# Folding a weight by seven half-block products a row pair, with sums and adds on GpSimd

## The chip, the cores and the metric

The kernel runs on one core of one Trainium2 chip. The metric is the device time of one execution in microseconds; the profile is one such execution, with a span of its own from the first to the last instruction.

## The reference

An mLSTM cell over 4 batches, 8 heads, 768 steps and a head width of 40, followed by a multiplicative feed-forward block on the cell's output, seen as 3072 tokens of width 320. All data are float32.

```python
# cell, for every step t (state C, n, m per batch and head)
m_new = np.maximum(f_gate[:, :, t] + m, i_gate[:, :, t])
f_stab = np.exp(f_gate[:, :, t] + m - m_new)
i_stab = np.exp(i_gate[:, :, t] - m_new)
C = f_stab * C + i_stab * einsum('bhd,bhe->bhde', vt, kt)
n = f_stab * n + i_stab * kt
y[t] = sigmoid(o_gate[t]) * einsum('bhde,bhe->bhd', C, qt) / max(|n . qt|, 1)
# feed-forward, x = y as (3072, 320)
a = x @ w1          # 320 x 1024
b = x @ w2
h = a * b @ w3      # 1024 x 1024
out = h @ w_out     # 1024 x 320
```

There is no nonlinearity between w3 and w_out, so the kernel folds the two: w3o = w3 @ w_out, 1024 x 320, and out = (a * b) @ w3o.

## The kernel before

The cell works on 24 blocks of 128 tokens (6 blocks of time times 4 batches), one a step `s`; the feed-forward block is spread over the same steps and eight more. The loop at L820 runs 32 steps. In a step stand, in program order: loads, the state's first decay (`decayed`, L333, GpSimd), the transposition of an older block's output into `xT` (`x_trans`, L478: TensorE transposes, ScalarE copies it out of the bank at L486), products with the folded weight where due (`fold`, `ffn_out`), the `up` blocks (a and b for two of the eight row blocks of w1 and w2, 256 tokens each), and the cell itself (`quarter_work`, L338). In the cell TensorE runs `up_rest` (the last 64 rows of the width), then the products of the cell, the first of which is `ph`; VectorE follows with the gating, the state's sums (L404, L414) and the output y (L445); GpSimd does the second decay between L404 and L414, then the weighted values of the next step (`weighted`, L327) and its masks (L308). At the end of a step two or three pieces of w3 are converted from raw words to float32 and transposed by VectorE (`convert`, L237, with L199, L200 and L248), ScalarE scales the next raw pieces (`scale_next`, L191 and L195; from step 9 on it keeps two scaled ones ready, L971), and SyncE issues the next loads, the raw pieces last (L184). There are four raw buffers (L179) and two for transposed rows of w3 (`w3T`, L247).

`x_trans` lags three steps behind in this part: in step 10 it turns block 7, in 12 block 9, in 14 block 11. The `up` blocks of steps 10 and 11 read blocks 6 and 7, those of 12 and 13 blocks 8 and 9, those of 14 and 15 blocks 10 and 11.

The fold is made by rows. A row `ko` is 128 rows of w3, complete in `w3T` after two conversions; a step later `fold` (L253) calls `w3_mm` (L259): eight products of 128 x 128 by 128 x 320 into one bank, which ScalarE empties into `w3o[:, ko]` (L264). Rows 0 and 1 come in step 10, then one a step up to row 7 in step 16. In steps 16 to 20 two output blocks a step follow (`ffn_out`, L733), whose copies to `o_sb` and stores are ScalarE's.

What sets the order: `in_order` (L84) chains all of TensorE's instructions in the order in which they are written. For the other engines `keep_order` (L549), called at the end of the last step (L979), chains every instruction traced after the front to the one before it on its engine. So all queues follow the program's text. [...]

Two other parts of the kernel already work by seven products in place of eight half-block ones: `up_by_seven` (L668, from step 19) and `out_by_seven` (L772, at the end).

Of the kernel before, what the change touches and what calls it, by code (L numbers as in the profile page):

```python
# [8 lines left out]
FP = mybir.dt.float32  # L9
U32 = mybir.dt.uint32  # L10
AF = mybir.ActivationFunctionType
OP = mybir.AluOpType
UP = 2.0 ** 9
# [3 lines left out]
def kernel(  # L17
# [26 lines left out]
    nc = tc.nc  # L44

    B, H, S, D = q.shape
    L = 64
    P = 128
# [6 lines left out]
    DM = H * D  # L55
    BH = B * H
    DFF = moe_w1.shape[1]
    FO = DFF // P
# [6 lines left out]
    const = ctx.enter_context(tc.tile_pool(name="const", bufs=1))  # L65
    wst = ctx.enter_context(tc.tile_pool(name="wst", bufs=2))
# [10 lines left out]
    def mps(shape, name):  # L77
        pool = banks.pop(0)
        banks.append(pool)
        return pool.tile(shape, FP, name=name, tag="m")  # L80

    last = []
# [8 lines left out]
    def mm(out, lhsT, rhs, start=True, stop=True):  # L91
        in_order(nc.tensor.matmul(out, lhsT=lhsT, rhs=rhs, start=start, stop=stop))  # L92
# [75 lines left out]
    wo = const.tile([128, FO, DM], FP, name="wo")  # L168
# [3 lines left out]
    w3o = const.tile([128, FO, DM], FP, name="w3o")  # L172
    CW = 512
# [35 lines left out]
    pend, scaled = [], []  # L209
# [18 lines left out]


    w3T_t = {}  # L230
    turned_w3, ready_w3 = [], []

    def scale_next(early=False):
        scaled.append(pend.pop(0))
# [2 lines left out]
    def convert():  # L237
        if not scaled:
            scale_next()
        dst, raw, ko, half = scaled.pop(0)  # L240
        if dst is not None:
            to_f32(dst, raw)
            return
        w3 = wst.tile([128, CW], FP, name="w3", tag="w3")
        to_f32(w3, raw)
        if half == 0:
            w3T_t[ko] = wst.tile([128, FO, 128], FP, name="w3T", tag="w3T")  # L247
        nc.vector.transpose(out=w3T_t[ko].rearrange("c k (m r) -> c m k r", r=32)[:, 2 * half:2 * half + 2],  # L248
                            in_=w3.rearrange("r (m c k) -> r m k c", m=2, k=FO))
        if half:  # L250
            turned_w3.append(ko)

    def fold():  # L253
        while ready_w3:
            w3_mm(ready_w3.pop(0))
        ready_w3.extend(turned_w3)
        turned_w3.clear()

    def w3_mm(ko):  # L259
        w3T = w3T_t.pop(ko)  # L260
        wp = mps([128, DM], "wp")
        for ki in range(FO):
            mm(wp, w3T[:, ki, :], wo[:, ki, :], start=(ki == 0), stop=(ki == FO - 1))
        nc.scalar.mul(out=w3o[:, ko, :], in_=wp, mul=UP ** -2)  # L264


    qT_t, kT_t, vw_t, before_t, y_t, x_t = {}, {}, {}, {}, {}, {}
# [227 lines left out]
    f_sb, a, F, U, on = (gates[0:RG, i * TC:(i + 1) * TC] for i in range(5))  # L495
# [99 lines left out]
    for i, r in enumerate(third):  # L595
        nc.gpsimd.tensor_tensor(out=pick[r, :, i, :], in0=pair[r].to_broadcast([BH, B * NP, GC]), op=OP.mult,
                        in1=dec[r].unsqueeze(1).to_broadcast([BH, B * NP, GC]))
# [15 lines left out]
    ffn = ctx.enter_context(tc.tile_pool(name="ffn", bufs=2))  # L613


    ab_t = {}

    def up(gr, fs, cs):


        if gr not in ab_t:
            ab_t[gr] = [ffn.tile([128, FO, 2 * P], FP, name="ab", tag="ab", bufs=6) for _ in range(2)]
        x, n = x_t[gr], cs.stop - cs.start
        pa, pb = mps([128, len(fs), n], "pa"), mps([128, len(fs), n], "pb")
        for p, wt in ((pa, w1), (pb, w2)):
            for i, f in enumerate(fs):
                for cc in range(KF):
                    mm(p[:, i, :], wt[:, cc, f * 128:(f + 1) * 128], x[:, cc, cs], start=(i == cc == 0), stop=False)
        return pa, pb, x, gr, fs, cs

    def up_rest(pa, pb, x, gr, fs, cs):
        for i, f in enumerate(fs):
            for j, e in quarters:
                mm((pa, pb)[j][halves[e], i, :], wr[halves[j], f * 128 + e * L:f * 128 + (e + 1) * L],
                   x[halves[j], KF, cs], start=False, stop=(i == len(fs) - 1))
        j, t0 = divmod(cs.start, 2 * P)
        a_sb = ffn.tile([128, len(fs), cs.stop - cs.start], FP, name="a_sb", tag="a_sb")
        nc.scalar.mul(out=a_sb, in_=pa, mul=UP ** -2)  # L638
        nc.vector.tensor_tensor(out=ab_t[gr][j][:, fs[0]:fs[-1] + 1, t0:t0 + a_sb.shape[-1]], in0=pb, in1=a_sb, op=OP.mult)  # L639
# [90 lines left out]

        return single, shared, left, product

    def ffn_out(blocks, pos=None):  # L733

        pos = pos or [mps([P, DM], "po") for _ in blocks]
        for (gr, j), po in zip(blocks, pos):
            for f in range(FO):
                mm(po, ab_t[gr][j // 2][:, f, j % 2 * P:(j % 2 + 1) * P], w3o[:, f, :], start=(f == 0), stop=(f == FO - 1))
        for (gr, j), po in zip(blocks, pos):
            o_sb = ffn.tile([P, DM], FP, name="o_sb", tag="o_sb", bufs=2)  # L740
            nc.scalar.copy(out=o_sb, in_=po)  # L741
            t0 = j * S + gr * P
            nc.scalar.dma_start(out=out[t0:t0 + P, :], in_=o_sb)


    KH, NH = FO // 2, DM // 2

    def out_weight_sums():

        T_o.extend(m[:, i * KH * NH:(i + 1) * KH * NH].rearrange("p (f n) -> p f n", n=NH)  # L750
                   for m, i in ((v_all, 0), (gates, 0), (gates, 1), (q_all, 0)))
        (B11, B12), (B21, B22) = ([w3o[:, k * KH:(k + 1) * KH, i * NH:(i + 1) * NH] for i in range(2)] for k in range(2))
        T1, T2, T3, T4 = T_o
        for dst, p, q in ((T1, B12, B11), (T2, B22, T1), (T3, B22, B12), (T4, B21, T2)):
            yield nc.gpsimd.tensor_tensor(out=dst, in0=p, in1=q, op=OP.subtract)

    T_o, S_o = [], {}
    wsums = out_weight_sums()

    def quarters_of_ab(gr, j):  # L760
        return [[ab_t[gr][j][:, k * KH:(k + 1) * KH, t * P:(t + 1) * P] for k in range(2)] for t in range(2)]
# [10 lines left out]
    def out_by_seven(gr, j, sums=None):  # L772
# [25 lines left out]
        for t in range(2):  # L798
# [3 lines left out]
    ups = [(gr, [f, f + 1], slice(j * 2 * P, (j + 1) * 2 * P)) for gr in range(3) for j in range(2)  # L802
           for f in range(0, FO, 2)]
    downs = [(gr, j) for gr in range(NG) for j in range(GT)][:14]
    outs = [(gr, j) for gr in range(3, NG) for j in range(2)][1:]
    summed = list(outs)
    sevens = [(gr, f) for gr in range(3, NG) for f in range(FH)]
    n_up = [0] * 2 + [1] * 4 + [2] * 10 + [0] * 16
    n_seven = [0] * 19 + [1] * 12 + [0]
    n_down = [0] * 16 + [2] * 5 + [1] * 4 + [0] * 7  # L810
# [9 lines left out]
    for s in range(len(n_up)):  # L820
# [28 lines left out]
        while s >= N_DVE and turned < min(s - 2, NY):  # L849
            x_trans(turned)  # L850
            turned += 1
        fold()
        if s >= len(n_up) - 2:
            ab_sums(*summed.pop(0))
        def pairs():
# [13 lines left out]
            seven[1]()  # L869
        if seven and s <= NU:  # L870
            ffn_out([downs.pop(0) for _ in range(n_down[s])], [cell[1][:, i, 0:DM] for i in range(2)])
        else:
            for _ in range(n_down[s]):
                ffn_out([downs.pop(0)])
# [2 lines left out]
        if seven and s > NU:  # L877
            seven[0]()
        now = [ups.pop(0) for _ in range(n_up[s])]
        open_ups = [up(*x) for x in now] if s != 2 else []  # L880
        if s == 3:
            turn(3)
        def rest():
            for x in open_ups:
                up_rest(*x)
            if seven:
                seven[2]()
            if s == 3:
                scale_next()
                scale_next()  # L890
# [23 lines left out]
        if s <= NU:  # L914
            gated = quarter_work(s, rest, between if s == 2 else None, convert if s == 3 else None)
        else:
            rest()
        with tc.issue_after(gated.ins) if gated else nullcontext():
            if seven:
                seven[3]()  # L920
            for _ in range({NU: 1, NU + 1: 3}.get(s, 0)):
                next(wsums)
            if s == NU + 1:
                ab_sums(*summed.pop(0))
            if NY <= s - 2 < NU:
                x_turn(s - 2)
            for n in () if s == 1 else (s + 2,) if s < B else (s + 2, s + 3) if s == B else (s + 3,):
                if n < N_U:
                    rows_of_u(n)
            if N_DVE <= s + 1 < NU:  # L930
                gated = turn(s + 1)
            if s - 2 in range(4 * GT - 1, NU, GT):
                token_sums((s - 2) // GT)
            if s < len(n_up) - 2 and n_out[s + 1] and s > NU + 2:
                ab_sums(*summed.pop(0))
# [28 lines left out]
        if s == B:  # L964
            for i, r in enumerate(third):
                nc.sync.dma_start(out=U_d[i * GC:(i + 1) * GC].rearrange("c r t -> r c t"), in_=U3[r])
        with tc.issue_after(gated.ins) if N_DVE <= s + 1 < NU else nullcontext():
            for _ in range(n_cvt[s] if s < len(n_cvt) else 0):
                convert()
                converted += 1  # L970
# [9 lines left out]
            for ins in keep_order(front):  # L980
                behind.enter_context(tc.issue_after(ins))
    behind.close()
    assert not ups and not sevens and not downs and not outs and not summed and not todo and not pend and not turned_w3 and not ready_w3, (len(ups), len(downs), len(todo), len(pend))
# [1 line left out]
_INS = ['q', 'k', 'v', 'i_gate', 'f_gate', 'o_gate', 'moe_w1', 'moe_w2', 'moe_w3', 'moe_w_out']  # L985
_OUTS = [((3072, 320), 'float32')]
# [25 lines left out]
```

## Time and profile before

| what | value |
|---|---|
| time, median of 3 runs | 427.91 us (426.82 to 428.42) |
| profiled execution | 427.89 us |
| its span | 425.8 us |
| granted clock, mean | 0.996 |
| ScalarE in a usual step (125.84 to 141.13 us, 15.29) | 6.50 us busy |
| VectorE in it | 12.24 us |
| GpSimd in it | 3.46 us |
| evacuation of a row of the fold (L264), 8 of them | 0.44 us each |

"PE" is TensorE's matmul row, "PEld" its weight loads, DVE VectorE, ACT ScalarE, POOL GpSimd, SP SyncE. A float32 product appears as two records. A record is drawn from its start to its modelled end, and records overlap, so the time that a group takes is read from the start of one group to the start of the next. "L92" is the line of the helper that all products go through; they are told apart by the names of what they write and read.

### The profile page before, as it was taken

What the parts mean: (1) busy time and instruction counts of PE and PEld (TensorE: products, weight loads), DVE (VectorE), ACT (ScalarE), POOL (GpSimd) and SP (SyncE); (2) the same over time, 40 slices, a digit from 0 to 9 for tenths busy, and PEclk for the clock granted to TensorE, in tenths of its full rate; (3) what the DMA queues carried; (4) which work ended last, traced back from release to release, by engine and by line L of the source; (5) the groups of instructions that cost most, each with busy time, mean ns of one, the idle gap of its engine ahead of it and who ended that gap; (6) DMA issues with size and microseconds to landing.
All of it is one profiled execution on the core that took longest, in us unless ns stands there. A gap on an engine that the chain in (4) does not pass through costs nothing.

```text
span 425.8 us, 13079 instructions
## 1 busy us (share of the span) xinstructions
PE 414.1 (97%) x5353; PEld 335.3 (79%) x5353; DVE 313.5 (74%) x635; ACT 150.1 (35%) x404; POOL 154.3 (36%) x211
## 2 busy tenths in 40 slices
PE   7989989999999999999999999999999999999996
PEld 4768878888688788787777778788778879888896
DVE  6676986888949779778736966596868699575971
ACT  4766865567723623630433313032311110210000
POOL 4421342233303303303307751546453587542100
PEclk9989999999999999999999999999999999999999
DMA  8999998598977776985425675756421120000001
GB/s 186 204 173 245 214 144 140 134 193 180 215 183 154 166 182 135 181 164 105 89 80 130 153 141 121 142 133 117 87 44 36 35 39 2 31 2 31 2 32 62
DMA packets 135211, 51.15 MB, mean 120 GB/s; under 512 B 109360, under 2 KB 126960, under 8 KB 135152
## 3 DMA queue, kind: packets, MB, share of 16 engines
q1 hardware_dynamic: 131552, 46.29, 53.9%
q10 hardware_dynamic: 3600, 4.03, 2.7%
q8 instruction: 42, 0.69, 0.7%
q14 instruction: 17, 0.14, 0.1%
HBM read 44.50 MB, written 5.80 MB: 118 GB/s over the span
## 4 chain that ended last, share of the span: by engine, by line
PE 53%; issue 20%; DVE 7%; POOL 7%; SPq 7%; DMA 5%; ACT 1%; POOLq 0%; DVEq 0%
PE cell L92 17%; PE pa L92 12%; PE o L92 8%; PE pb L92 8%; PE p L92 3%; POOL pw L308 3%; SPq L184 3%; DVE w3T L666 2%; PE pt L95 1%; POOL vw L330 1%; SPq L148 1%; DMA raw<-in_moe_w_dram 1%; PE fill L92 1%; POOL raw L659 1%; POOL state L335 1%
## 5 line engine op out<-in xcount | busy, mean ns | idle before, releaser
L335 POOL TENSOR_TENSOR state<-state,decay 128x164 f32<-128x164 f32 x40 | 20.0, 500 | 154.8 <-DVE state L404 129.0
L92 PE MATMUL pa<-xT,w 128*128 128x256 f32 x240 | 60.4, 382 | 0.0
L92 PEld LDWEIGHTS pa<-xT,w 128*128 128x128 f32 x240 | 44.4, 190 | 6.8 <-DVE h L430 0.4
L303 ACT ACTIVATE pw<-pw,aT 128x64 f32<-128x64 f32 x184 | 46.4, 339 | 3.2 <-ACT o_sb L741 1.9
L92 PE MATMUL pb<-xT,w 128*128 128x256 f32 x192 | 45.4, 379 | 0.0
L729 POOL TENSOR_TENSOR ab<-ab,a_sb 128x512 f32<-128x512 f32 x22 | 29.4, 1356 | 32.2 <-DVE ab L684 32.2
L92 PEld LDWEIGHTS pb<-xT,w 128*128 128x128 f32 x192 | 36.4, 190 | 5.0
L711 POOL TENSOR_TENSOR wo<-wo 128x512 f32<-128x512 f32 x22 | 27.4, 1268 | 29.8 <-DVE wo L686 29.8
L92 PE MATMUL pa<-xT,wr 64*64 64x256 f32 x384 | 37.0, 386 | 0.5 <-DVE wr L200 0.5
L92 PE MATMUL wp<-wo,w3T 128*128 128x320 f32 x128 | 35.9, 433 | 1.1 <-DVE ab L639 0.6
L308 POOL TENSOR_SCALAR_AFFINE_SELECT pw<-pw 64x512 f32<-64x512 f32 x48 | 35.8, 746 | 3.0 <-ACT pw L303 1.2
L92 PE MATMUL pb<-xT,wr 64*64 64x256 f32 x384 | 36.4, 380 | 0.0
L92 PE MATMUL cell<-w3o,ab 128*128 128x320 f32 x128 | 35.4, 432 | 0.0
L638 ACT ACTIVATE a_sb<-pa 128x512 f32<-128x512 f32 x24 | 14.3, 598 | 59.0 <-PE pb L92 59.0
L639 DVE TENSOR_TENSOR ab<-pb,a_sb 128x512 f32<-128x512 f32 x24 | 16.4, 688 | 23.2 <-ACT a_sb L638 22.8
L92 PEld LDWEIGHTS wp<-wo,w3T 128*128 128x128 f32 x128 | 23.8, 190 | 10.5 <-DVE ab L639 0.8
L92 PEld LDWEIGHTS cell<-w3o,ab 128*128 128x128 f32 x128 | 24.3, 190 | 9.5
L92 PEld LDWEIGHTS pa<-xT,wr 64*64 64x64 f32 x384 | 18.9, 132 | 15.4 <-issue 8.8
L686 DVE SCALAR_TENSOR_TENSOR a_sb<-pa,wo 128x512 f32<-128x512 f32 x12 | 8.3, 689 | 29.8 <-PE pa L92 29.8
L430 DVE TENSOR_TENSOR h<-cell,h 64x164 f32<-64x164 f32 x88 | 28.6, 326 | 1.6
L92 PE MATMUL po<-w3o,ab 128*128 128x320 f32 x96 | 26.4, 433 | 0.0
L92 PEld LDWEIGHTS po<-w3o,ab 128*128 128x128 f32 x96 | 18.1, 190 | 7.3
(180 smaller groups left out, 846.4 us busy)
## 6 DMA issues: line engine op xcount, KB each, us to landing
raw<-in_moe_w_dram SPq DMA_DIRECT2D x64, 128.0 KB, 3.4
kbuf<-in_k_dram SPq DMA_DIRECT2D x24, 160.0 KB, 4.5
v_all<-in_v_dram SPq DMA_DIRECT2D x24, 160.0 KB, 4.9
o_in<-in_o_gate_dram SPq DMA_DIRECT2D x24, 160.0 KB, 4.8
pw<-U_d SPq DMA_DIRECT2D x28, 128.0 KB, 3.5
raw<-in_moe_w_dram SPq DMA_DIRECT2D x5, 512.0 KB, 6.7
raw<-in_moe_w_out_dram SPq DMA_DIRECT2D x8, 320.0 KB, 4.1
gates<-in_k_dram SPq DMA_DIRECT2D x28, 80.0 KB, 2.5
```

What stands on the lines that cost most here:

```text
L92: in_order(nc.tensor.matmul(out, lhsT=lhsT, rhs=rhs, start=start, stop=stop))
L184: nc.sync.dma_start(out=dst, in_=src)
L303: nc.scalar.activation(out=pw[:, h, :], in_=src[:, h, :], func=AF.Exp, bias=aT[:, c, b * H + h:b * H + h + 1])
L308: nc.gpsimd.affine_select(out=pw[r], in_=pw[r], compare_op=OP.is_ge, fill=0.0, base=0, pattern=[[0, H], [1, L]], channel_multiplier=-1)
L335: nc.gpsimd.tensor_tensor(out=new, in0=old, op=OP.mult, in1=decay[:, b * NP:(b + 1) * NP, 2 * c + x:2 * c + x + 1] .to_broadcast([P, NP, D1]))
L430: nc.vector.tensor_tensor(out=part, in0=ph[x][halves[e]], in1=part, op=OP.add)
L638: nc.scalar.mul(out=a_sb, in_=pa, mul=UP ** -2)
L639: nc.vector.tensor_tensor(out=ab_t[gr][j][:, fs[0]:fs[-1] + 1, t0:t0 + a_sb.shape[-1]], in0=pb, in1=a_sb, op=OP.mult)
L666: nc.vector.tensor_tensor(out=dst, in0=p, in1=q, op=OP.subtract)
L686: nc.vector.scalar_tensor_tensor(out=out, in0=p, scalar=UP ** -2, in1=q, op0=OP.mult, op1=OP.add)
L711: aside_by.tensor_tensor(out=kept[j][:, 1:4:2], in0=kept[j][:, 1:3], in1=kept[j][:, 3:4].to_broadcast([128, 2, TH]), op=OP.add)
L729: aside_by.tensor_tensor(out=t[:, f:FO:FH, :], in0=t[:, f:FO:FH, :], in1=a, op=OP.mult)
```

## The change

The eight row products a row of w3 are replaced. Two rows (2i and 2i + 1) and the two column halves of w_out make a 2 x 2 by 2 x 2 product of blocks, and this is made with seven products of half blocks in place of eight. The sums of w_out's blocks (T1, T2, T4, and B22 - B12 in place of B12) are made once, those of a row pair (S1, S2, S4, and S3 in place of A21) for each pair, all on GpSimd, and so are the five adds that put the products together; ScalarE alone empties the banks.

- Steps 8 and 9: two sums of w_out each, on GpSimd, after the cell.
- Steps 9, 11, 13, 15: `fold_sums` of a pair on GpSimd after the cell; at the end of the step, ahead of the conversions, `fold_first`: two products and their emptying. In step 15 it also rebuilds T4 in B21's place.
- Steps 10, 12, 14: the first `up` of the step with its rest, then `fold_second`: the other five products and two emptyings; then the second `up`. The adds are issued on GpSimd after the cell.
- Step 16: `ffn_out` is split: six of the eight f for both blocks, then `fold_second(3)` with its adds, and after the cell the other two f and the stores.
- `w3` has one buffer in place of two; `o_sb` lies in the memory of T1; group 2's `ab` is taken in step 9, its memory serves the sums meanwhile; the last pair's sums use two raw buffers.

```diff
-        w3 = wst.tile([128, CW], FP, name="w3", tag="w3")
+        w3 = wst.tile([128, CW], FP, name="w3", tag="w3", bufs=1)
...
-    def w3_mm(ko):
-        w3T = w3T_t.pop(ko)
-        wp = mps([128, DM], "wp")
-        for ki in range(FO):
-            mm(wp, w3T[:, ki, :], wo[:, ki, :], start=(ki == 0), stop=(ki == FO - 1))
-        nc.scalar.mul(out=w3o[:, ko, :], in_=wp, mul=UP ** -2)
+    def fold_weight_sums():
+        (B11, B12), (B21, B22) = halves_of(wo)
+        T1, T2, T4 = (m.rearrange("p (f n) -> p f n", n=NH) for m in
+                      (fold_m[:, 0], fold_m[:, 1], w3o[:, FO - 2:FO].rearrange("p k n -> p (k n)")))
+        fold_T.extend((T1, T2, B12, T4))
+        for dst, p, q in ((T1, B12, B11), (T2, B22, T1), (T4, B21, T2), (B12, B22, B12)):
+            yield nc.gpsimd.tensor_tensor(out=dst, in0=p, in1=q, op=OP.subtract)
+
+    def fold_sums(i):
...
+        (A11, A12), (A21, A22) = rows_of_w3(i)
+        S1, S2, S4 = (m.rearrange("p (k r) -> p k r", r=128) for m in mem)
+        fold_S[i] = S1, S2, A21, S4
+        fold_M[i] = mem[1], mem[2]
+        for dst, p, q, op in ((S1, A21, A22, OP.add), (S2, S1, A11, OP.subtract), (A21, A11, A21, OP.subtract),
+                              (S4, A12, S2, OP.subtract)):
+            nc.gpsimd.tensor_tensor(out=dst, in0=p, in1=q, op=op)
+
+    def fold_first(i):
+        (A11, A12), _ = rows_of_w3(i)
+        (B11, _), (B21, _) = halves_of(wo)
+        wp = fold_products(((A11, B11), (A12, B21)))
+        if i == FO // 2 - 1:
+            nc.gpsimd.tensor_tensor(out=B21, in0=B21, in1=fold_T[1], op=OP.subtract)
+            fold_T[3] = B21
+        nc.scalar.mul(out=fold_of(i)[:, 0:3:2], in_=wp, mul=UP ** -2)
+
+    def fold_second(i):
...
+        wp, wq = mps([128, 3, NH], "wp"), mps([128, 2, NH], "wq")
+        for p, x, a, b, first, last in ((wq, 1, A22, T4, True, False), (wp, 0, S1, T1, True, False), (wp, 1, S2, T2, False, False),
+                                        (wp, 2, S3, T3, False, True), (wq, 0, S4, B22, False, True)):
+            for k in range(KH):
+                mm(p[:, x], a[:, k, :], b[:, k, :], start=(first and k == 0), stop=(last and k == KH - 1))
+        M1, M2 = (m[:, 0:n * NH].rearrange("p (x n) -> p x n", n=NH) for m, n in zip(fold_M[i], (3, 2)))
+        nc.scalar.mul(out=M1, in_=wp, mul=UP ** -2)
+        nc.scalar.mul(out=M2, in_=wq, mul=UP ** -2)
+
+        def adds():
+            for out, p, q in ((C[:, 1], M1[:, 1], C[:, 0]), (C[:, 0], C[:, 0], C[:, 2]), (C[:, 2], M1[:, 2], C[:, 1]),
+                              (C[:, 1:4:2], C[:, 1:3], M1[:, 0:1].to_broadcast([128, 2, NH])), (C[:, 1:3], M2, C[:, 1:3])):
+                nc.gpsimd.tensor_tensor(out=out, in0=p, in1=q, op=OP.add)
+        return adds
...
-        fold()
...
+        elif s == 16:
+            finish = ffn_out([downs.pop(0) for _ in range(n_down[s])], split=FO - 2)
+            fold_second(FO // 2 - 1)()
...
         now = [ups.pop(0) for _ in range(n_up[s])]
-        open_ups = [up(*x) for x in now] if s != 2 else []
+        open_ups, adds = [], []
+        if s in (10, 12, 14):
+            up_rest(*up(*now.pop(0)))
+            adds.append(fold_second((s - 10) // 2))
+        if s != 2:
+            open_ups = [up(*x) for x in now]
...
+        if s == 16:
+            finish()
         with tc.issue_after(gated.ins) if gated else nullcontext():
             if seven:
                 seven[3]()
+            if s in (8, 9):
+                next(fsums), next(fsums)
+            for x in adds:
+                x()
+            if s in (9, 11, 13, 15):
+                fold_sums((s - 9) // 2)
...
+        if s in (9, 11, 13, 15):
+            fold_first((s - 9) // 2)
         with tc.issue_after(gated.ins) if N_DVE <= s + 1 < NU else nullcontext():
             for _ in range(n_cvt[s] if s < len(n_cvt) else 0):
                 convert()
```

## The prediction

> **What bounds the kernel now.** I read the page first, then the waits of TensorE (PE), the groups by shape, stretches by step, and the timeline of ScalarE (ACT), VectorE (DVE), GpSimd (POOL) and SyncE (SP) from 90 to 236 us. The page's busy line and groups (line, engine, op, out<-in, shapes, count | busy us, mean ns | idle before):
>
> ```profile
> PE 414.1 (97%) x5353; PEld 335.3 (79%) x5353; DVE 313.5 (74%) x635; ACT 150.1 (35%) x404; POOL 154.3 (36%) x211
> L92 PE MATMUL wp<-wo,w3T 128*128 128x320 f32 x128 | 35.9, 433 | 1.1 <-DVE ab L639 0.6
> L335 POOL TENSOR_TENSOR state<-state,decay 128x164 f32<-128x164 f32 x40 | 20.0, 500 | 154.8 <-DVE state L404 129.0
> ```
>
> PE is the bound: everything issued on it is in one fixed order (`mm`, L92), so time taken out of PE shortens the run, and each wait of PE lengthens it. GpSimd idles 12 us a step, but in its queue's order: the idle ends at the state's decay, and what follows the decay can't start before it. Steps 9 to 15 are told apart by the first product of the cell (ph), at 105.40 (step 9), 125.84, 141.13, 157.12, 172.40, 187.69 and 202.98 us (15); I call that moment q. A usual step is 15.29 us: one w3 row (16 records from 128.04 to 132.35, 4.31) and 10.98 of the rest, of which two `up` blocks take 8.78 (117.06 to 125.84).
>
> The timeline of the stretch that decides (start us, us, engine, line, op):
>
> ```profile
> 107.22 0.55 PE L95 MATMUL px<-ident,y 128*128 128x128 f32 x3
> 108.35 8.88 PE L92 MATMUL wp<-wo,w3T 128*128 128x320 f32 x32 [0.58 <-DVE ab L639]
> 110.80 0.68 ACT L191 ACTIVATE raw<-raw 128x512 f32<-128x512 f32 x1 [1.17 <-DMA raw<-in_moe_w_dram]
> 113.04 0.68 ACT L191 ACTIVATE raw<-raw 128x512 f32<-128x512 f32 x1 [1.01 <-DMA raw<-in_moe_w_dram]
> 115.07 0.69 ACT L191 ACTIVATE raw<-raw 128x512 f32<-128x512 f32 x1 [0.78 <-DMA raw<-in_moe_w_dram]
> 116.22 0.46 ACT L486 COPY xT<-px 128x384 f32<-128x384 f32 x1
> 117.06 1.89 PE L92 MATMUL pa<-xT,w 128*128 128x256 f32 x8
> ```
>
> The block of tokens turned at 107.22 is copied out of its bank only at 116.22: ScalarE keeps program order, and ahead of the copy stand the scalings of four raw w3 tiles, three of which wait for their DMA. PE doesn't notice: two w3 rows (8.71 us) lie between. The next `up` reads that block (step 10's tokens 256 to 511 hold block 7) and begins 0.38 us after the copy. So the w3 products are not only work; they are the cover of that copy.
>
> [...]
>
> **The change, part by part.**
>
> *Products removed and added.* Out: 8 rows x 4.31 = 34.5 us of PE, and two small gaps beside them (0.58 shown above, 0.54 of issue at 144), 35.6. In: 4 pairs x 7 products x 4 blocks x 2 records = 224 records of 160 columns. The output products of that shape at the end take 23.03 us for 168 in the chain, 0.137 each: 30.7. Gain 3.8, with the gaps 4.9. A pair is 7.67: two first products 2.19, five second ones 5.48.
>
> *Where they are put.* The first two products come at the end of steps 9, 11, 13, ahead of the next transposition (px); the other five come after the first `up` of steps 10, 12, 14. Between px and that `up` nothing is left. These are just the steps that need the new block: 10 needs block 7, 12 block 9, 14 block 11 (`x_trans` lags by three steps). In steps 11, 13 and 15 the blocks are old, no wait.
>
> *Step 10.* Cell ends 107.22, first products to 109.41, px to 109.80. On ScalarE the new emptying (0.44, after 109.6) fits ahead of the waits for DMA, and the scalings end as before with L486 at 116.22 to 116.68, since SP's queue and the raw buffers aren't touched up to there. PE goes on at about 116.9: **7.1 us idle**. Then up 4.31, five products, up: q(10) = 131.2, against 125.84.
>
> *Steps 12 and 14.* The steps before them are now short: q(11) = q(10) + 10.98. From q(11) px ends at 1.82 + 2.19 + 0.39 = 4.40. ScalarE: exponentials and gate to 3.1, emptying of the first products 4.2 to 4.64, then two scalings, the second of them on a tile whose DMA waits for a buffer that VectorE frees 12.0 after q(10) (L200 at 137.17 + 0.69 in the trace). Its last issue is at q(10) + 13.35; landing to scaling took 4.2 for the three tiles above (110.86 to 115.07): q(11) + 6.57. Then two activations at 0.56 and the copy 0.46: 8.15, PE at 8.35. **3.95 us each**, 3.1 if the DMA isn't late; I take 3.95.
>
> *Step 16.* Here two blocks of output products (24 records at 0.269, 6.46) cover the copy. But `fold_first(3)` rebuilds T4 on GpSimd behind the decay, the sums, the weighting and the masks of step 15, and `fold_second(3)` starts with T4. VectorE needs 13.0 us from q(14) (125.84 to 139.01, less a little), the step is 10.98, so its chain in step 15 is 2.0 late. GpSimd: decay 4.53 + 2.0 to 6.95; four sums of 512 at 1.27 to 1.36 (L659, L711, L729): 12.2; weighting 0.73, masks 1.77: 14.65; T4 of 640 at 1.55 to 2.0 (L755): 16.5. PE wants it at 1.82 + 2.19 + 0.39 + 6.46 = 10.86: **5.7 us**; 3.7 without the lag.
>
> *The last adds.* Rows 6 and 7 are wanted by `finish` one cell (1.82) after the fifth product. ScalarE's emptying, then three adds of 160 (0.47 like the 164 of L335), two of 320 (0.75, L330): 2.75 + 0.2 late: **1.1 us**.
>
> *Hidden.* T1, T2 in step 8 and T4, B12 in step 9 (4 x 1.5 to 2.0), the sums (4 x 5.2) and the adds (3 x 2.9): GpSimd has 12 us a step. Queued behind them are weighting and masks of the next step: step 10's weighting is then done at about 123, needed at 132; in a short step the adds delay it to q + 8.6, needed at q + 12.3. If that cover were gone, PE would wait for vw at once. Step 10's S4 is ready at about 122, used at 125.6. VectorE's transposition of row 2 must wait for S4 (its buffer is row 0's), 117.1 to 122; behind it stands the evacuation of the first `up`, done 126, needed at 128. ScalarE: 0.6 us more a pair, of 9 spare. The o_sb tiles move into T1's memory: same copies, same DMAs. The w3 single buffer: VectorE only, in order.
>
> *The clock.* The 7.1 and 5.7 us gaps may each cost from 0 to 1.7 us (the loss of the stretch 20 to 30: 10 x 0.17). I take 0.9 in all, keeping 0 and 3.4.
>
> **Sum.** -4.9 + 7.1 + 3.95 + 3.95 + 5.7 + 1.1 + 0.9 = +17.8 on the profiled execution's 427.89 (span 425.8 and 2.1 around it), which is the median of the runs, 427.91, within 0.02: **445.7**.
>
> **Rivals.**
> - *Engines take what is ready.* If the copy L486 and T4 pass ahead of the scalings and masks, PE waits 0.7 to 0.9 at steps 10, 12, 14, nothing for T4, 0 to 1.1 for the adds: -4.9 + 2.2 = 425.2 or so, 423.0 with no wait. Faster. It decides as soon as all waits together stay below 4.9 us. Against it: not one ScalarE or GpSimd instruction from 90 to 236 stands out of program order, and the code chains them all at the last step (`keep_order(front)`). 0.10.
> - *T4 comes in time*, as VectorE isn't late or the GpSimd sums run faster: -5.7 and some clock, 439. For: the 2.0 lag is a difference of two sums. Against: even without it 3.7 stay. 0.20.
> - *The clock falls at each gap*: four times 1.7 instead of 0.9, and VectorE slower beside GpSimd: 450.5. [...] 0.15.
> - *Forecast*, 441 to 448: 0.55. That the products aren't shortened as written I leave out: the output stage shows the shape at its price.
>
> The likeliest holds 0.55; with the second rival's bulk and the lower part of the third the range is 434 to 450. Faster by over 0.5% (2.1 us, about what a measurement can tell) 0.07, within 0.03, slower 0.90.
>
> **What would show it.** PE wp records of 0.137 and 224 of them; idle of PE before `pa` in three places, released by ACT xT L486; idle before `wq` in step 16 released by POOL wo; q(11) - q(10) near 11 and q(10) - q(9) near 25.8. If PE stays 97% busy, or L486 runs right behind px, I am wrong, and the time is near 425.

## The result and the profile after

The changed kernel takes **456.56 us** (median of four runs, 454.23 to 458.17) where the kernel before takes 428.17 beside it: a ratio of **1.0691, interval 1.0637 to 1.0745**. The prediction said 445.7 and 434 to 450. The sign and the places were right, the size was short by 11 us.

The profiled execution took 455.23 us, its span is 453.5 us, the mean granted clock 0.977 (before 0.996). The page of the changed kernel:

```profile
span 453.5 us, 13332 instructions
PE 420.5 (93%) x5449; PEld 347.4 (77%) x5449; DVE 326.2 (72%) x635; ACT 151.7 (33%) x408; POOL 202.2 (45%) x252
...
PEclk9999999999699699999988999999999999999999
```

PE's share fell from 97% to 93%, so there are waits now. But its busy time *rose* by 6.4 us, though the change takes out products worth 3.8. The third line, PEclk, explains it: two slices show a clock of 0.6 and two of 0.8 (each digit is the clock in tenths over a fortieth of the span), and at half the clock a group counts as busy for twice the time (the eight records of `pa` below: 3.78 us, 1.89 before). Before, that row has a single 8, in another place. The products of the fold answer to the row of 128 records at 433 ns shown of before (a group of the tile wp of the changed kernel: min/median/max in ns, first and last start):

```profile
L92 PE MATMUL wp<-wo,w3T x96: 299/299/403, 105.2 to 238.2; 128*128 128x160 f32 x96
```

The row length is halved as the code says. Where PE stands still, from its waits (what it waited for: us in total, times, longest):

```profile
PE pa L92 <- ACT xT L548: 13.2, 3, 6.4
PE wq L92 <- POOL wo L301: 4.6, 1, 4.6
PE cell L92 <- issue: 1.7, 3, 0.7
PE px L95 <- issue: 1.7, 1, 1.7
...
PE po L92 <- POOL w3o L322: 1.4, 1, 1.4
```

The three waits for `xT` (steps 10, 12, 14), the one for T4 and the one for the last adds are the five of the forecast; the longest wait before was 1.6 us. The first of them in the timeline of the changed kernel, in selected lines (start, us, engine, line, op, idle before):

```profile
105.24 2.44 PE L92 MATMUL wp<-wo,w3T 128*128 128x160 f32 x16
107.95 0.55 PE L95 MATMUL px<-ident,y 128*128 128x128 f32 x3 [0.27 <-DVE ab L701]
111.01 0.66 ACT L191 ACTIVATE raw<-raw 128x512 f32<-128x512 f32 x1 [0.66 <-DMA raw<-in_moe_w_dram]
113.28 0.67 ACT L191 ACTIVATE raw<-raw 128x512 f32<-128x512 f32 x1 [1.07 <-DMA raw<-in_moe_w_dram]
114.40 0.46 ACT L548 COPY xT<-px 128x384 f32<-128x384 f32 x1
114.91 3.78 PE L92 MATMUL pa<-xT,w 128*128 128x256 f32 x8 [6.42 <-ACT xT L548]
```

The copy of the turned block starts at 114.40, 10.98 us after q(9) = 103.42; before it started 10.82 after. It hasn't moved, and PE has nothing to do until it ends. Then comes what the forecast took for small: `pa` takes 3.78 us for eight records that took 1.89 before.

The time from q to q (the first product of the cell), in us; "forecast" is by the prediction's steps without its 0.9 for the clock:

| steps | before | after | forecast | idle in it, after |
|---|---|---|---|---|
| 9 to 10 | 20.44 | 28.76 | 25.8 | 6.42 xT, 0.27 bank of px |
| 10 to 11 | 15.29 | 10.98 | 10.98 | none |
| 11 to 12 | 15.99 | 26.44 | 22.6 | 3.93 xT, 0.29 issue |
| 12 to 13 | 15.28 | 12.87 | 10.98 | 1.67 issue |
| 13 to 14 | 15.29 | 22.12 | 22.6 | 2.86 xT |
| 14 to 15 | 15.29 | 10.99 | 10.98 | none |
| 15 to px of 17 | 17.09 | 31.25 | 27.1 | 4.58 T4, 1.45 adds, 0.73 issue |

The steps sum to 114.7 before and 143.4 after, +28.7; the front is 2.0 shorter and the tail 0.9 longer, which makes the +27.7 of the span. Most of the front's gain is not the change's: the stretch at half clock at 23.41 to 26.83 us of before, worth 1.7 us, is missing after, and it comes and goes in runs of the kernel before too (mean clock 0.996 or 1.0).

**How the clock goes.** The stretches at half clock begin and end on a raster of 3.41 us: cut along it, all thirteen profiles show a clock of 1.00 or 0.50 in every window from about 20 to 400 us, and nothing between. Where the raster begins differs from one execution to the next (edges at 23.41 us in the profile before, at 113.36 in this one). With the raster's windows as stretches, the changed kernel shows (stretch, length, busy us and records of PE, PEld, DVE, ACT, POOL, then PEclk, DMA share, GB/s):

```profile
109.94:113.36 3.42, 0.00 (x0) 0.00 (x0) 2.91 (x8) 1.70 (x4) 1.89 (x2) 1.00 0.93 223
113.36:116.77 3.41, 1.86 (x4) 1.52 (x5) 3.38 (x4) 1.50 (x3) 3.33 (x3) 0.50 1.40 174
116.77:120.18 3.41, 3.41 (x9) 2.70 (x8) 3.09 (x3) 0.00 (x0) 3.41 (x3) 0.50 0.58 142
120.18:123.60 3.42, 3.42 (x31) 2.51 (x30) 2.19 (x3) 0.60 (x1) 3.27 (x6) 1.00 0.55 155
...
147.49:150.90 3.41, 0.80 (x7) 0.56 (x5) 2.83 (x11) 1.85 (x4) 0.69 (x2) 1.00 0.77 190
150.90:154.32 3.42, 2.10 (x5) 1.75 (x6) 3.38 (x4) 1.26 (x3) 3.34 (x3) 0.50 1.12 175
154.32:157.73 3.41, 3.41 (x9) 2.69 (x9) 3.24 (x5) 0.00 (x0) 3.41 (x4) 0.50 0.45 116
...
185.03:188.45 3.42, 2.03 (x16) 1.79 (x14) 2.84 (x12) 2.21 (x6) 0.82 (x2) 1.00 0.84 190
188.45:191.86 3.41, 1.94 (x9) 1.74 (x10) 3.38 (x4) 1.42 (x3) 3.33 (x3) 1.00 0.88 166
191.86:195.27 3.41, 3.41 (x30) 2.41 (x29) 3.24 (x5) 0.55 (x1) 3.41 (x4) 1.00 0.55 152
...
229.41:232.82 3.41, 0.63 (x4) 0.63 (x5) 0.00 (x0) 0.00 (x0) 3.19 (x5) 1.00 0.56 134
232.82:236.24 3.42, 3.42 (x15) 3.42 (x14) 0.00 (x0) 0.00 (x0) 0.00 (x0) 0.50 0.00 0
...
239.65:243.06 3.41, 1.96 (x129) 1.85 (x126) 2.24 (x7) 0.39 (x1) 2.87 (x5) 1.00 0.02 5
243.06:246.48 3.42, 3.42 (x7) 2.21 (x8) 2.92 (x8) 0.42 (x1) 1.16 (x2) 0.50 0.00 0
```

To be read downwards: a window in which PE is busy for 0.00, 0.80 or 0.63 us is followed by one at 0.50; the clock comes back after a full one (3.41) and not after 1.86 or 2.10. Step 14 keeps its clock although its gap is 2.86 us: the gap falls across two windows and leaves 2.03 and 1.94 us of work in them. That is luck of the raster, and a near thing: the window at 239.65, with 1.96 us of work, was followed by half clock. So a window with 0.80 us of work in it was idle enough.

Six windows at half clock cost half of 6 x 3.41, less half of the idle time in them (1.55 and 1.32), which I count as not lengthened: by this estimate 10.2 - 1.4 = **8.8 us**. The mean clock says the same: 6 x 1.707 / 453.5 = 0.0226, and 1 - 0.0226 = 0.977. The other three executions were granted 0.963, 0.970 and 0.970; by the same reckoning, an estimate, they had about ten, eight and eight such windows. So the number of windows isn't the kernel's alone, and the profiled execution had the fewest.

The trace before held a first sign of this (the same columns):

```profile
20.00:23.41 3.41, 2.23 (x52) 1.75 (x52) 2.81 (x8) 2.38 (x8) 2.14 (x4) 1.00 1.22 165
23.41:26.83 3.42, 3.42 (x29) 1.92 (x31) 3.04 (x9) 2.78 (x6) 0.53 (x2) 0.50 0.96 146
```

The loss of 0.17 that the prediction takes over the ten microseconds from 20 to 30 (the mean clock there is 0.83) is one window at half clock, and PE's idle time in the window ahead of it is one wait of 1.19 us (`px` for y, up to 22.96). The same wait, 0.99 to 1.19 us long, stands in all thirteen profiles, and in four of them half clock follows: before, the place alone, the w3 buffer alone, and the copy behind `fold_first`.

### The profile page after: what moved, and what is told of

The parts are those of the page before. It is cut to its first block, busy times and chain, and to the rows that moved or that the text cites. A ratio compares the mean times of both kernels' runs of the same rounds, so it can differ in the third digit from the quotient of the medians.

```text
span 453.5 us, 13332 instructions
## 1 busy us (share of the span) xinstructions
PE 420.5 (93%) x5449; PEld 347.4 (77%) x5449; DVE 326.2 (72%) x635; ACT 151.7 (33%) x408; POOL 202.2 (45%) x252
## 4 chain that ended last, share of the span: by engine, by line
PE 58%; DVE 9%; SPq 8%; DMA 8%; issue 8%; POOL 6%; ACT 3%; DVEq 0%; POOLq 0%; ACTq 0%
PE cell L92 16%; PE pa L92 15%; PE pb L92 9%; PE o L92 8%; DMA raw<-in_moe_w_dram 4%; PE p L92 4%; SPq L139 4%; PE wp L92 3%; SPq L184 2%; PE wq L92 2%; DVE w3T L728 1%; SPq L153 1%; POOL pw L370 1%; DMA wo<-in_moe_w_dram 1%; DMA o_in<-in_o_gate_dram 1%
## 5 line engine op out<-in xcount | busy, mean ns | idle before, releaser
L92 PE MATMUL pa<-xT,w 128*128 128x256 f32 x240 | 64.3, 401 | 13.4 <-ACT xT L548 13.2
L92 PEld LDWEIGHTS pa<-xT,w 128*128 128x128 f32 x240 | 45.9, 199 | 21.4 <-ACT xT L548 13.9
L92 PE MATMUL pb<-xT,w 128*128 128x256 f32 x192 | 47.4, 391 | 1.1 <-DVE w L200 1.1
L92 PEld LDWEIGHTS pb<-xT,w 128*128 128x128 f32 x192 | 38.0, 198 | 7.2 <-DVE w L200 1.5
L492 DVE TENSOR_TENSOR h<-cell,h 64x164 f32<-64x164 f32 x88 | 28.7, 326 | 1.7
L92 PE MATMUL po<-w3o,ab 128*128 128x320 f32 x96 | 28.4, 455 | 1.4 <-POOL w3o L322 1.4
L485 DVE TENSOR_TENSOR h<-cell,gT 128x328 f32<-128x328 f32 x24 | 11.8, 491 | 21.9 <-PE cell L92 21.9
L392 POOL TENSOR_TENSOR vw<-v_all,wT 128x328 f32<-128x328 f32 x24 | 19.5, 811 | 6.3 <-DMA v_all<-in_v_dram 4.7
```

The costliest lines, as they stand in the source:

```text
L392: nc.gpsimd.tensor_tensor(out=vw_t[n], in0=vbuf[n % NBV], op=OP.mult, in1=wT[:, c, b * H:(b + 1) * H].unsqueeze(2).to_broadcast([P, H, D1]))
L485: nc.vector.tensor_tensor(out=h.rearrange("p (n two) d -> p two n d", two=2), in0=pi, in1=gT[:, c, hs].rearrange("p (n two) -> p two n", t ...
L492: nc.vector.tensor_tensor(out=part, in0=ph[x][halves[e]], in1=part, op=OP.add)
```

## The experiments

Ratios are to the kernel before, timed on the same chip beside the version. The kernel before took 428.17 us beside the changed kernel and 425.4 to 426.5 beside the versions, so a difference in us from the changed kernel's 456.56 is sure to about 2 us only; the ratios compare better. Sums that a version adds without use, and filling products, change nothing in what is computed.

**The place alone.** The kernel before, its eight products a row kept, with both rows of a pair behind the first `up` of steps 10, 12, 14 and the last two in step 16. No sums, no seven products.

```diff
     def fold():
-        while ready_w3:
-            w3_mm(ready_w3.pop(0))
-        ready_w3.extend(turned_w3)
-        turned_w3.clear()
+        while len(turned_w3) > 1:
+            w3_mm(turned_w3.pop(0))
+            w3_mm(turned_w3.pop(0))
...
-        fold()
+        if s == 16:
+            fold()
...
         now = [ups.pop(0) for _ in range(n_up[s])]
+        if s in (10, 12, 14):
+            up_rest(*up(*now.pop(0)))
+            fold()
```

> The kernel before, with its eight products a row, only put where the changed kernel has its fold: both rows of a pair after the first up of steps 10, 12 and 14, rows 6 and 7 in step 16; no sums and no adds. Theory (the place is the cause): waits of 8.6, 6 and 5 us before the first up, plus three stretches of half clock at 3.4: 428 + 30 = about 455 to 459. Rival (the seven-product scheme is the cause): 428 to 433.

454.64 us, **1.0681 (1.0631 to 1.0730)**: as slow as the whole change. PE's waits in it:

```profile
PE pa L92 <- ACT xT L485: 14.9, 2, 8.7
PE pa L92 <- DVE o_in L442: 5.6, 1, 5.6
```

They are 8.66 (step 10), 5.56 and 6.25 (12 and 14), each ahead of the first `up`, and seven windows in steps 10 to 14 are at half clock. (The second line is a wait for the copy too: the copy ends at 155.76, 0.01 us before the operation that the view names.) In the changed kernel the two first products stand ahead of px and shorten these waits. So the place, without the seven products and GpSimd's sums, is enough for a loss of this size. That both come to 1.07 is chance in part: this version waits 20.5 us for the copy where the changed kernel waits 13.2, and has no T4 and no adds to wait for. In the changed kernel's trace the waits for the copy and the half clock in their steps make 13.2 + 5.4 = 18.6 us, the waits for T4 and the adds with theirs 6.0 + 3.4 = 9.4, both GpSimd's.

**GpSimd's share alone.** The kernel before with sums of the same sizes at the change's places, their results unused, and one w3 buffer; then the buffer alone; then the sums without those of step 8. (The lines that make `spare` and the single buffer are left out here.)

```diff
+            if s in (8, 9):
+                dead = w3o[:, FO - 2:FO].rearrange("p k n -> p (k n)").rearrange("p (f n) -> p f n", n=NH)
+                for m in (0, 1):
+                    nc.gpsimd.tensor_tensor(out=dead, in0=wo[:, 4 * m:4 * m + 4, 0:NH], in1=wo[:, 4 - 4 * m:8 - 4 * m, 0:NH], op=OP.subtract)
+            if s in (10, 12, 14, 16):
+                for n in (160, 160, 160, 320, 320):
+                    nc.gpsimd.tensor_tensor(out=spare[:, 0:n], in0=spare[:, 0:n], in1=spare[:, 512 - n:512], op=OP.add)
+            if s in (9, 11, 13, 15):
+                for m in range(4):
+                    nc.gpsimd.tensor_tensor(out=spare, in0=spare, in1=wo[:, 0:2].rearrange("p f d -> p (f d)")[:, 0:512], op=OP.subtract)
```

> The kernel before, with as many GpSimd sums of the same sizes put at the changed kernel's places in steps 8 to 16 and their results unused; the w3 buffer single as in the changed kernel. Theory (GpSimd's work is hidden, and slows VectorE only where PE doesn't wait for it): ratio to before 0.998 to 1.005. Rival (the sums' contention with VectorE costs time of its own): over 1.01, 4 us and more.

431.50 us, **1.0130 (1.0072 to 1.0188)**: I had called these sums hidden, and they are not. The profile of this version, VectorE and GpSimd in step 8, then PE in step 10; below it VectorE in step 8 of the kernel before:

```profile
95.01 3.31 POOL L926 TENSOR_TENSOR w3o<-wo 128x640 f32<-128x640 f32 x2
95.33 1.57 DVE L444 SCALAR_TENSOR_TENSOR o_in<-o_in,den 128x320 f32<-128x320 f32 x1
96.93 1.74 DVE L446 TENSOR_TENSOR y<-h,o_in 128x320 f32<-128x320 f32 x1
...
107.57 10.57 PE L92 MATMUL wp<-wo,w3T 128*128 128x320 f32 x32 [2.80 <-DVE ab L641]
```

```profile
98.35 0.76 DVE L443 SCALAR_TENSOR_TENSOR o_in<-o_in,den 128x320 f32<-128x320 f32 x1
99.15 0.49 DVE L445 TENSOR_TENSOR y<-h,o_in 128x320 f32<-128x320 f32 x1
```

Beside GpSimd's two sums VectorE's two products take 1.57 and 1.74 us; in the kernel before they took 0.76, beside the end of a weighting on GpSimd, and 0.49, beside an idle GpSimd. VectorE is about 2 us late from there on, the evacuation that frees a bank for the fold in step 10 is late, PE waits 2.80 us instead of 0.58, and the window after has half the clock: 10.57 us for 32 records that took 8.88.

> The kernel before with only the single w3 buffer of the change. Theory (VectorE alone uses it, in order): no difference, ratio 0.997 to 1.003. Rival (this, and not GpSimd's sums, made VectorE late in the run with the sums alone): 1.01 or more.

The buffer alone, `bufs=1`: 426.18 us, 1.0008 (0.9979 to 1.0037), no cost that shows. The next edit is to the version with the sums:

```diff
-            if s in (8, 9):
+            if s in (9,):
```

> The kernel before with the unused GpSimd sums, but without the two of step 8. Theory (the sums of step 8 slow VectorE's conversions, which holds the emptying that step 10's row waits for, and the half clock follows): the wait of 2.8 us and some 2 of half clock go, ratio 1.003 against 1.013. Rival (the cost is spread over all the sums): still 1.01.

427.33 us, 1.0048 (1.0027 to 1.0069); the wait in step 10 is 0.93. So the larger part of what the sums cost in this stand-in is the pair in step 8. The stand-in isn't like the changed kernel everywhere: in both versions with unused sums PE waits 1.8 us for VectorE at the start of step 19, where it waits 0.4 in the kernel before and in the changed one. Why stays open.

**The clock alone.** The changed kernel with products of no use in the gaps ahead of the first `up` of steps 10, 12, 14 (8, 5, 4 of them). The waits stay as long; only PE is busy in them.

```diff
         if s in (10, 12, 14):
+            warm({10: 8, 12: 5, 14: 4}[s])
             up_rest(*up(*now.pop(0)))
```

> 8, 5 and 4 idle identity products of 512 columns are put between px and the first up of steps 10, 12 and 14; all else is as in the changed kernel. If the half clock comes from PE's idleness: the 6.9 us that it costs behind the first two waits go, less 1.5 of products that outlast the waits: about 451. If the slow products have another cause (weights, contention on memory), nothing goes and the fill adds 0 to 1.5: 456 to 458.

447.90 us, **1.0515 (1.0466 to 1.0564)**: 8.7 us less than the change, 7.5 by the ratios. The window of this version over step 10 shows the full clock:

```profile
104.00:131.00 27.00, 26.21 (x291) 19.95 (x287) 19.89 (x29) 10.21 (x24) 12.61 (x12) 1.00 0.77 174
```

The steps are 26.87, 10.98, 23.29, 10.98, 23.28, 10.98. Steps 10 and 12 gain 1.9 and 3.2. Step 13 gains 1.9, as its idle time is gone; step 14, whose clock had not fallen, loses 1.2 of that again, as its copy starts 8.08 us after q(13) and not 6.93: behind a short step the scaling ahead of it waits 0.98 for its tile. 1.9 more lie between q(15) and the px of step 17 (29.31 against 31.25), where one window at half clock is left of two, and 0.9 behind it. So the clock itself shows cleanly in steps 10 and 12 alone: 5.1 us gained, where the four windows at half clock are reckoned at 5.4. With the clock held in these three steps the time lies 2.2 us from my forecast, which had little of it.

**T4 alone.** T4 of the last pair is made in a raw buffer of its own, ahead of the pair's other sums and not behind the masks.

```diff
+            own = wst.tile([128, CW, 2], U32, name="raw", tag="raw", bufs=4).rearrange("p n two -> p (n two)").bitcast(FP)
+            own = own[:, 0:2 * DM].rearrange("p (f n) -> p f n", n=NH)
+            nc.gpsimd.tensor_tensor(out=own, in0=halves_of(wo)[1][0], in1=fold_T[1], op=OP.subtract)
+            fold_T[3] = own
...
-        if i == FO // 2 - 1:
-            nc.gpsimd.tensor_tensor(out=B21, in0=B21, in1=fold_T[1], op=OP.subtract)
-            fold_T[3] = B21
```

> T4 of the last pair is rebuilt into a raw buffer of its own, ahead of the four sums of step 15, not behind the masks. Theory: the wait of 4.6 us for T4 in step 16 goes, and the half clock behind it (some 2 to 3.5 us): 456.6 to about 449.5. Rival (the last S sum or the late VectorE sets that step anyway): within 2 us of 456.6.

450.19 us, **1.0571 (1.0525 to 1.0618)**: 6.4 less than the change, 5.1 by the ratios. The wait of 4.58 is gone and with it one window at half clock, 1.7: together 6.3. In the changed kernel it stood so (timeline, GpSimd and PE in step 16):

```profile
229.15 1.37 POOL L370 TENSOR_SCALAR_AFFINE_SELECT pw<-pw 64x512 f32<-64x512 f32 x2
230.61 1.53 POOL L301 TENSOR_TENSOR wo<-wo,fold_m 128x640 f32<-128x640 f32 x1
232.19 1.92 PE L92 MATMUL wq<-wo,w3T 128*128 128x160 f32 x8 [4.58 <-POOL wo L301]
242.88 4.11 PE L92 MATMUL po<-w3o,ab 128*128 128x320 f32 x8 [1.45 <-POOL w3o L322]
```

**The copy early, in two places.** The block's transposition and copy at the end of steps 9, 11 and 13, ahead of the new first products, so that on ScalarE no scaling stands before it.

```diff
+        if s in (9, 11, 13):
+            x_trans(turned)
+            turned += 1
         if s in (9, 11, 13, 15):
             fold_first((s - 9) // 2)
```

> The turned block is transposed and copied to xT at the end of steps 9, 11 and 13, ahead of the first two products and of the scalings. Theory (PE waits for that copy, and each wait is followed by a stretch at half clock): the waits of 6.4, 3.9 and 2.9 us go, and with them two stretches that cost 3.4 each, 456.6 - 20 = about 437, with the T4 wait of step 16 left. Rival (the seven products slow the step through GpSimd, VectorE and the emptying of banks, and the waits only show where): under 5 us gained, above 451.

439.64 us, **1.0344 (1.0275 to 1.0413)**. The waits for xT are gone, and a new one stands in their place. The timeline of this version:

```profile
105.47 0.55 PE L95 MATMUL px<-ident,y 128*128 128x128 f32 x3
108.58 4.11 PE L92 MATMUL wp<-wo,w3T 128*128 128x160 f32 x16 [2.56 <-DVE ab L701]
```

The kernel hands out four PSUM banks in turn to px, `wp` and the `up` blocks (`mps`). px now takes the bank that comes free early and `wp` the next, which VectorE frees at 108.5, late behind step 8's sums. The sixteen records, 2.44 us in the changed kernel, then take 4.11 at half clock.

So the same three lines behind `fold_first`, ahead of the scalings:

```diff
         if s in (9, 11, 13, 15):
             fold_first((s - 9) // 2)
+        if s in (9, 11, 13):
+            x_trans(turned)
+            turned += 1
```

> The changed kernel with the transposition and copy of the block moved to the end of steps 9, 11 and 13 behind the first two products, still ahead of the scalings. Only ScalarE's order changes; PE's is the same. Theory: each of the three waits shrinks to about 0.9 us (transposition's end to the copy's end) and no stretch at half clock follows: 456.6 - 13.5 + 2.7 - 6.9 = about 438 to 439, a little under the version with the copy ahead of the products. Rival (something else holds the first up): above 445.

441.79 us, **1.0370 (1.0323 to 1.0417)**, 3 more than expected. The xT waits are 0.57 each: product, copy, product in a row with nothing between. But in step 10 PE is now at the pair's second products earlier than GpSimd's sums S are there (1.65 us, and a window at half clock behind it), and 2.04 us are lost ahead of px in step 13.

**All mended.** That, T4 early, and the second products in another order (those that need T4 and S4 last).

```diff
-        for p, x, a, b, first, last in ((wq, 1, A22, T4, True, False), (wp, 0, S1, T1, True, False), (wp, 1, S2, T2, False, False),
-                                        (wp, 2, S3, T3, False, True), (wq, 0, S4, B22, False, True)):
+        for p, x, a, b, first, last in ((wp, 0, S1, T1, True, False), (wp, 1, S2, T2, False, False), (wp, 2, S3, T3, False, True),
+                                        (wq, 1, A22, T4, True, False), (wq, 0, S4, B22, False, True)):
```

> The copy behind the first two products but ahead of the scalings, T4 of the last pair rebuilt early into a buffer of its own, and the three products of the wide bank first in the second five, so that the adds can start earlier. Theory: the two repairs add up (18 and 6.4 us) and the last wait falls under 0.5: 430 to 432, against 427 before: with all large waits gone the 3.8 us of products saved are spent on the three short waits of 0.9, the wait for the adds and issue gaps. Rival (the waits hide one another): the gains overlap, above 435.

437.30 us, **1.0284 (1.0236 to 1.0332)**, 5 to 7 more than expected. The two longest of its PE waits in these steps:

```profile
PE wp L92 <- POOL ab L288: 2.9, 1, 2.9
PE po L92 <- POOL w3o L323: 2.0, 1, 2.0
```

With the large waits gone PE comes sooner to the next pieces of GpSimd's chain: 2.93 us for the sums of the first pair (the new order also takes away the products that stood ahead of this wait) and 1.97 for the last adds, each with half clock behind it. By the medians the repairs nearly add up: 14.8 and 6.4 us alone, 19.3 together with the new order, a difference within the 2 us above. The expectation fell short in good part because it counted 18 for the copy.

**Two pairs instead of four.** Rows 2 to 5 by seven products, where GpSimd has time; rows 0, 1, 6 and 7 by eight; the copy early and the order as above. The edit's main lines:

```diff
+        for ko in {10: (0, 1), 15: (6,), 16: (7,)}.get(s, ()):
+            w3_mm(ko)
...
-            if s in (8, 9):
+            if s in (9, 10):
...
-            if s in (9, 11, 13, 15):
+            if s in (11, 13):
                 fold_sums((s - 9) // 2)
```

> Seven products for rows 2 to 5 only (two pairs), with the copy ahead of the scalings and the wide bank first; rows 0, 1, 6 and 7 by eight products at the places of the kernel before, so that step 10 keeps its cover and step 16 its order. The sums of w_out are made in steps 9 and 10. Theory (each pair saves 1.0 us and pays 0.6 for the copy, some more where GpSimd slows VectorE): within 1% of before, 425 to 430. Rival (the short steps themselves, in which VectorE is late, cost more): over 432.

437.73 us, 1.0267 (1.0236 to 1.0298), outside what I expected. It waits 8.18 us in step 15 for B12, which this version has to restore on GpSimd behind the adds of step 14: a fault of the version, not of the scheme. Moved one step:

```diff
-        for ko in {10: (0, 1), 15: (6,), 16: (7,)}.get(s, ()):
+        for ko in {10: (0, 1), 16: (6, 7)}.get(s, ()):
```

> As the version with two pairs, only row 6 moved from step 15 to step 16 beside row 7, past the restoring of B12 on GpSimd that held it for 8.2 us (that wait was a mistake of the version, not of the scheme). Theory: the 8.2 and some 3.5 of half clock behind it go, 437.7 - 11.7 = 426; by the steps (83.4 us from step 9 to step 14 for six rows, against 82.3 and 4.3 for the sixth row before) it may come out 3 us under the kernel before, ratio 0.992 to 1.000. Rival (the late VectorE of the short steps shows elsewhere): over 1.005.

430.20 us, **1.0101 (1.0064 to 1.0138)**, again above what I expected. The two pairs of steps that use seven products take 31.9 and 30.8 us against 31.3 and 30.6 before: no gain. In step 16 two short waits, 1.07 and 0.88, fall in one window with 1.50 us of work in it, and the next is at half clock. No version beat the kernel before.

## Why the prediction was wrong in its size

- **What bounds it, and the place**: right. The copy of xT stands where it stood, and what had covered it is gone. The place alone gives 1.0681, and the copy made early (441.79 us, PE's order unchanged) takes 14.8 us off.
- **Products, -4.9**: by the prices of the rows the steps without any wait come to 109.3 against 114.7, -5.3. The records have the expected length, 299 ns drawn and 0.137 us in a chain (5 x 8 in 5.48). But with waits and clock taken off, steps 10 and 12 are 0.8 longer than the rest of the step and the pair's products, steps 14 and 16 0.6 (22.12 - 10.98 - 7.67 - 2.86 in step 14), step 13 0.2: 3.0 in all, over half of the gain. The version with the place alone has 0.6 in each of steps 10, 12 and 14 too, with eight products a row (29.13 - 10.98 - 8.62 - 6.25 - 2.70 of clock in step 14). So most of it goes with the place and not with the seven products. PE changes between the small and the full tiles more often in these steps; that this is the reason was not tested.
- **Waits, 21.8 forecast** (7.1, 3.95, 3.95, 5.7, 1.1): 19.5 measured (6.7 with the bank, 3.93, 2.86, 4.58, 1.45). Step 14 waits less because step 13 was 1.9 longer and the tile was no longer late; in the version with filled gaps, where step 13 takes 10.98, 4.0 us lie between px and `pa`. GpSimd's queue in step 16 was as worked out: T4 ended at q(15) + 16.56, forecast 16.5. PE came later to these places than forecast by the gaps below. (In the sum of step 10 one `up` block is entered as 4.31; by 8.78 for two it is 4.39, and the 131.2 stands.)
- **The clock, +0.9**: **this is the step that failed**. It measured 8.8. I counted the 7.1 and the 5.7 us gap alone, at 0 to 1.7 each; no run shows this term of 0.9. What the runs showed in its place: a window need not be empty (0.80 and 0.63 us of work did not save it), the 3.93 us gap was enough, a gap can cost two windows, since the one in which PE resumes is not full, and even 1.45 us behind the cell cost one. The trace before could have warned me: I read its loss as 0.17 spread over ten microseconds, where one wait of 1.19 us stands ahead of a whole window at half clock. My rival with four falls at 1.7 was the right mechanism, at a chance of 0.15, and too small still; its own terms sum to 445.7 - 0.9 + 6.8 = 451.6, not the 450.5 written. Filling the gaps holds the full clock (1.00 in every window) through steps 10 to 14, which shows that PE's idleness brings the half clock; the 8.7 us that it gave back are not the same sum as these 8.8, as they hold other gains too.
- **Issue gaps**, 0.29 + 1.67 + 0.73 = 2.7: in no step of mine. The profile shows nothing that PE waits for there; in the version with filled gaps the 1.67 is gone, in another there are 2.04 us in the same place, put down to a VectorE operation. This stays open.
- **GpSimd's sums hidden**: wrong. Alone, at the old places, they cost 1.3%, the larger part through VectorE's products in step 8. In the changed kernel that shows only as 0.27 at px, since the longer wait for xT comes behind it; it is 2.56 when that wait is taken away.

The sum on the steps: -5.3 + 19.5 + 8.8 + 2.7 + 3.0 = 28.7, as measured. With the forecast's terms and the measured clock in place of 0.9 the time would have been 445.7 + 7.9 = 453.6, against 455.2 in the profiled execution. That it comes so near is luck in part: the 5.7 us of the last two terms, in no step of mine, are offset by 2.3 less of waits and a front that is 2.0 shorter.

## What to carry to other kernels

Before products are moved, ask what copies they cover: on an engine with a fixed order the copy stays behind what is queued ahead of it, and taking the work out from over it cost more here than the work saved. Price a gap of TensorE by the clock's windows and not by its length alone. By what the thirteen profiles of this case show: lay a raster of 3.41 us over it, in its best and its worst place, since it is not known beforehand; after a window with at most 1.13 us of work (from 1.49 to 2.29 it is uncertain) add 1.7 us for each window until one with 2.92 us of work or more has passed, less half of the idle time in it. And where several waits stand in a row on one chain, removing the first shows the next: look for it before you count the gain.

## What the runs showed of the hardware

- **A short gap halved the clock, and a longer one left it.** Half clock followed the wait of 1.19 us at the start of the kernel before, and none followed the 2.86 us of step 14 in the changed kernel. In the thirteen profiles every window from about 20 to 400 us with at most 1.13 us of PE's busy time was followed by half clock. From 1.49 to 2.29 us it went both ways, and busy time alone doesn't decide there: with little but the cell's small products in it, a window with 1.96 us (at 239.65 in the changed kernel) fell and one with 1.89 us (in the version with the copy behind `fold_first`) held. What decides in this band stays open. The clock came back after windows of 2.92 us of work (in the version with filled gaps) or more; 2.76 (in the version with all mended) was not enough.
- **VectorE beside GpSimd's sums.** In step 8, while sums of 128 x 640 ran on GpSimd, VectorE's products of 128 x 320 took 1.57 and 1.74 us in the version with the sums alone, and 1.57 and 1.73 in the changed kernel:

```profile
95.40 1.55 POOL L266 TENSOR_TENSOR fold_m<-wo 128x640 f32<-128x640 f32 x1
95.72 1.57 DVE L505 SCALAR_TENSOR_TENSOR o_in<-o_in,den 128x320 f32<-128x320 f32 x1
97.03 1.69 POOL L266 TENSOR_TENSOR fold_m<-wo,fold_m 128x640 f32<-128x640 f32 x1
97.33 1.73 DVE L507 TENSOR_TENSOR y<-h,o_in 128x320 f32<-128x320 f32 x1
```

  Each VectorE operation starts beside a GpSimd operation and ends 0.34 us after it. In the traces of before and after, 25 of these two products ran with GpSimd idle, and all took 0.49 us; 71 started beside a running GpSimd operation, and all ended 0.34 to 0.35 us after it, whether that operation took 0.5 or 1.8 us in all. So beside GpSimd their price here was what was left of its operation and 0.35 us. Beside a mask it was 0.82 us, for the y product at 131.91 of before.
